# A gated two-branch spectral filter on one core: narrow gate spectra, swaps on the load queue, an inverse in four buffers

## Chip, core and metric

One core of one Trainium2 chip. The metric is device time in microseconds of one launch. A run of the profiler gives the trace that is read here; the times come from runs without it and from that run.

## The reference

`x` is 2048 x 1024 in bf16; `A_w`, `B_w` are complex weights of 2048 x 513; `gate_w` has 1024 elements.

```python
g = sigmoid((x * gate_w).sum(-1, keepdims=True))
a = irfft2(rfft2(x) * (A_w_r + 1j * A_w_i))
b = irfft2(rfft2(x) * (B_w_r + 1j * B_w_i))
return g * a + (1 - g) * b
```

Both branches share the input and its spectrum.

## The kernel before

The transforms are matrix products in seven stages, in one hand-written order. `P.add` records an instruction for one engine with the keys that it reads and writes; each engine's instructions run in the order in which they were recorded, and every DMA has a semaphore of its own. SP issues the loads, ACT issues two small ones. RP is one large buffer of four slots (A0, A1, S0, S1), XF holds spectra.

- Stage 1 (`c` = 0 to 7, two halves `j` each): x in eight pieces of two DMAs, times the constant M, into XF by evictions on ACT or DVE (EV1). x lies in slot A0, M in slot S1.
- The gate needs the sum of x times `gate_w` over a row. It is taken from stage 1's output: `zspec` multiplies XF by the small vectors GS (made from `gate_w`), a DVE product (L411) multiplies the result by the constant E, and `zsum` (L417) adds it up into ZS. `gates` then spreads ZS by matmuls and `sigmoids` (L607) evicts them into FZ. E and the product's result TE also lie in slot S1.
- Stages 2 and 4, for eight row groups `i` (four rows of tiles each): stage 2 is 16 matmuls of 256 columns into PSUM banks 0 to 3, evicted to CG; stage 4 is 8 of 512 columns into banks 4 to 7, evicted to X(i) in XF. The order is 2(0), 2(1), 4(0), 2(2), 4(1) and so on to 2(7), 4(6), 4(7). ACT evicts, with DVE taking half where EVC and EVX name the group.
- The products: `prods(i0, i1, c0, c1)` multiplies, on DVE, spectrum by weights for row groups i0 to i1 and columns c0 to c1. It needs X, and X with even and odd partitions exchanged (a "swap", two DMAs within SBUF into slot S1). For the groups in NSW no swap of X is made; the weights are there in both forms instead.
- Weights: `load_w` lists the loads, `issue_w` issues them on SP. W0 is how many are issued at once; `issue_late` issues those whose place is still in use by x, M or E.
- Stage 5, the inverse over k: 16 units of two column groups `g`, each group 16 matmuls; a unit fills four banks, which ACT evicts in one piece (the call at L648); the last unit is split between ACT and DVE (EV5). Products of later columns are put on DVE between the units (PRODS5), `column0` in front of unit 6 (NCOL0), the unit with groups 0 and 1 at place G0, and `gated` and `rbgen`, which put the gate on the constant U5, near the end.
- Stages 6 and 7, for `r` = 0 to 15: 16 matmuls and an eviction, then the inverse over columns, either whole (8 matmuls of 512 columns, two DVE sums) or, for `r` in FOUR, in quarters (8 of 256 columns, three sums on DVE and one on POOL), and the output DMA.

Before, the swaps of X are issued by POOL (XSQ), and each waits for the sum of the gate:

```python
if i not in NSW:
    for pa in range(2):
        dma(XSQ, sl(RP, S_S1 + 4 * i * RW, [(1, 4 * RW)], p0=pa, np_=64, step=2),
            sl(XF, 4 * i * RW, [(1, 4 * RW)], p0=1 - pa, np_=64, step=2), r=[("X", i), "pad"],
            w=[] if pa else [("XS", i)], a=[("XS", i)] if pa else [], after=[s1, zs[1]] + P.rd["E"])
```

L300 is the line of every matmul, L304 and L305 those of the evictions on ACT and on DVE, L308 that of the products, L291 that of every DMA, L540 that of `rbgen`, L675 that of the sums in stage 7.

Of the kernel before, what the change touches and what calls it, by code (L numbers as in the profile page):

```python
# [4 lines left out]
dt = mybir.dt  # L5
# [23 lines left out]
def make_consts():  # L29
# [23 lines left out]
    E = np.zeros((4, 32, 4, 16, 2, 2, 8))  # L53
    for q in range(4):
        for b in range(2):
            for r in range(8):
                n2 = 32 * b + 8 * q + r
                for t in range(16):
                    if t == 0:
                        re, im = np.ones(32), (-1.0) ** n1  # L60
                    else:
                        ph = pi2 * t * (64 * n1 + n2) / 2048
                        re, im = 2 * np.cos(ph), -2 * np.sin(ph)
                    E[n2 // 16, :, q, t, 0, b, r], E[n2 // 16, :, q, t, 1, b, r] = re / 32, im / 32
    C["E"] = E.reshape(128, 2048)

# [156 lines left out]
def bass_gated_mix__spectral_gfnet__spectral_gfnet__prompt_kernel(nc, A_x, A_w_r, A_w_i, B_x, B_w_r, B_w_i, gate_w, out):  # L223
# [32 lines left out]
    W0 = 36  # L256
    XSQ = "pool"
    NSW = (6, 7)
    ZAT = {5: (0,), 7: (1, 2)}
    ZAT2 = {0: (3,)}  # L260
    ZBANK = (6, 7, 6, 7)
    PRODS = [[], [], [(0, 2, 0, 64)], [(0, 2, 64, 128)], [(2, 4, 0, 64)], [(2, 4, 64, 128)], [(4, 5, 0, 64), (5, 6, 0, 64)], [(6, 7, 0, 64), (7, 8, 16, 32), (7, 8, 32, 64), (7, 8, 0, 16)]]
    PRODS5 = {0: [(4, 8, 64, 128)], 1: [(0, 8, 128, 160)], 2: [(0, 8, 160, 208)], 3: [(0, 8, 208, 248)], 4: [(0, 8, 248, 256)]}
# [12 lines left out]
    POOL7 = range(16)  # L276
    EV5 = (15,)
# [15 lines left out]
    def bank(b):  # L293
        return ("ps", b)
# [18 lines left out]
    MO, MN, EO, TEO = 16, 4112, 8224, 10272  # L313
# [16 lines left out]
    P.add("pool", lambda e: e.memset(sl(XF, 512, [(RW, 32), (1, 16)]), 0.0), w=["pad"])  # L330
    P.add("act", lambda e: e.activation(XST[:, 0:1], sl(XF, 512, [(1, 1)]), ACT.Sigmoid), r=["pad"], w=["XST0"])
# [8 lines left out]
    dma("sp", sl(RP, S_S1 + EO, [(1, 2048)]).bitcast(u16), cst["E"].ap(), w=["E"])  # L340
# [14 lines left out]
    wlist, wlate = [], []  # L355

    def issue_w(n):
        for _ in range(min(n, len(wlist))):
            dst, src, key = wlist.pop(0)
            dma("sp", dst, src, w=[key])  # L360

    def issue_late():
        for dst, src, key in wlate:
            dma("sp", dst, src, w=[key], after=[s1] if key[1] == S_A0 else zs)

    def load_w(t0, n, groups, swapped):

        todo = []
        for f in range(2):
            for ri in range(2):  # L370
                todo.append((f, ri, S_S0 if f == 0 and not swapped else S_A1 if f else S_A0, ri))
                if swapped:
                    todo.append((f, ri, S_S1 if f else S_S0, 1 - ri))
        todo.sort(key=lambda x: x[2] == S_A0)
        for f, ri, base, pa in todo:
            for pm in range(2):
                w = wsrc[f, ri]
                spans = [(t0, n)] if pm == 0 or t0 else [(0, 1), (1, n - 1)]
                for a, m in spans:
                    k1, st = (a, 513) if pm == 0 else (16, 513) if a == 0 else (32 - a, -513)  # L380
                    dst = sl(RP, base + (2 * a + pm) * RW, [(2 * RW, m), (1, 513)], p0=pa, np_=64, step=2)
                    key = ("W", base, pa, pm, a)
                    late = base == S_A0 or base == S_S1 and a < 14
                    (wlate if late else wlist).append((dst, AP(w.tensor, w.offset + k1 * 513, [[32 * 513, 64], [st, m], [1, 513]]), key))
                    for g in groups:
                        wkeys.setdefault(g, []).append(key)

    lo = min(NSW + (8,))
    for g in range(4):
        i0, i1 = 2 * g, min(2 * g + 2, lo)  # L390
        if i0 < i1:
            load_w(2 * i0, 2 * (i1 - i0), range(i0, i1), False)
        if i1 < 2 * g + 2:
            i1 = max(i1, i0)
            load_w(2 * i1, 2 * (2 * g + 2 - i1), range(i1, 2 * g + 2), True)

    issue_w(W0)
    load_ck(*cks[1])
# [4 lines left out]
    def zspec(q):  # L403

        o = ZBANK[q] * 512
        for j in range(2):
            for f in range(4):
                mm(ps(o, [(1, 512)]), sl(GS, 4 * j + f, [(0, 128)]), sl(XF, j * RW + f * 128 + 8 * q, [(2 * RW, 16), (32, 4), (1, 8)]),
                   j == 0 and f == 0, j == 1 and f == 3, ["GS"] + F1[2 * q:2 * q + 2], [bank(ZBANK[q])])
        te = sl(RP, S_S1 + TEO + ((q % 2) * 1024 + (q // 2) * 512) * 2, [(1, 1024)]).bitcast(dt.float32)  # L410
        return P.add("dve", lambda e: e.tensor_tensor(out=te, in0=ps(o, [(1, 512)]), in1=sl(RP, S_S1 + EO + 512 * q, [(1, 512)]), op=ALU.mult),  # L411
                     r=["E", bank(ZBANK[q])], a=[("TE", q % 2)])

    def zsum(q):
        te = sl(RP, S_S1 + TEO + q * 2048, [(1, 2048)]).bitcast(dt.float32)
        src = AP(te.tensor, te.offset, [list(te.ap[0]), [1, 8], [8, 128]])
        return P.add("dve", lambda e: e.tensor_reduce(ZS[:, 8 * q:8 * q + 8], src, mybir.AxisListType.X, ALU.add),  # L417
                     r=[("TE", q)], a=["z"])
# [8 lines left out]
    for c in range(8):  # L427
        if c < 7:
            reverse(c + 1)
        for j in range(2):  # L430
            k = 2 * c + j
            u = k % 3
            for q in range(4):
                r = 4 * c + q
                o = ps(u * 1024 + q * 256, [(1, 256)])
                mo = S_S1 + MO + r * 128
                mm(o, sl(RP, S_A0 + r * 512 + 128 * j, [(1, 128)]), sl(RP, mo, [(8, 16), (0, 2), (1, 8)]), True, False,
                   [("x", c, 0), ("x", c, 1), ("M", MK[c])], [bank(2 * u + q // 2)])
# [5 lines left out]
        for q in ZAT.get(c, ()):  # L444
            zspec(q)
# [18 lines left out]
    def stage4(i):  # L464
# [52 lines left out]
    for what, i in order:  # L517
        if what == "2":
            stage2(i)
            for q in ZAT2.get(i, ()):  # L520
                zspec(q)
            if i == 0:
                zs += [zsum(0), zsum(1)]
                issue_w(len(wlist))
                issue_late()
            continue
# [89 lines left out]
    units = [[g, g + 1] for g in range(2, 32, 2)]  # L616
    units.insert(G0, [0, 1])
    lowlast = max(n for n, gs in enumerate(units) if gs[0] < 16)
    for n, gs in enumerate(units):
# [6 lines left out]
        u = (n + 1) % 2  # L626
        if n == NCOL0:
            column0(4 * u)
        for g in gs:
            if n == 0 and g == gs[1]:  # L630
                gates(12, 4, 0)
                sigmoids(12, 4, 0)
            for q in range(8):
                l0 = 8 * g + q
                for ab in range(2):
                    deps = [("PS" if ab else "PA", g), "CK2"]
                    if g == 0:
                        deps.append(("col0", ab))
                    if g == 31:
                        deps.append(("c256", ab))  # L640
                    w = l0 - 8 * gs[0]
                    last5 = mm(ps(u * 2048 + w * 128, [(1, 128)]), sl(RP, (S_S0 if ab else S_A0) + l0, [(HW, 128)]),
                               sl(CK, KIBo if ab else KIAo, [(1, 128)]), ab == 0, ab == 1, deps, [bank(4 * u + w // 4)])
        if n == lowlast:
            half5 = last5
        parts = [(0, 16)] if n not in EV5 else [(0, 8), (8, 8)]
        for a, cn in parts:
            move("dve" if a else "act", sl(RP, S_A0 + 8 * gs[0] + a, [(HW, 128), (1, cn)]), ps(u * 2048 + 128 * a, [(1, 128), (128, cn)]),  # L648
                 r=banks(4 * u + a // 4, cn // 4), a=["L4"])
# [134 lines left out]
```

## Time and profile before

| | before |
|---|---|
| median of 3 runs (lowest, highest) | 154.51 us (154.02, 154.75) |
| profiled execution | 154.8 us |
| its span, first to last instruction | 152.6 us |
| mean granted TensorE clock | 0.954 |
| busy: PE, DVE, ACT, POOL | 125.3, 104.2, 94.4, 30.0 us |
| DMA | 28.31 MB, mean 185 GB/s |

A row of the timeline or the chain begins with start and length in microseconds; brackets hold the idle time before it and what ended it. A row of a group ends with busy time, mean ns of one, and the idle time before them with its releasers. `SPq` is SP's DMA queue. A row of windows has, behind the five engines' busy times, the granted clock (1.00 is full), the DMA engines' share and GB/s.

### The profile page before, as it was taken

Reading aid. Unit: us, or ns where it says so; the run is one execution under the profiler, and the core shown is the slowest. Engines: PE = TensorE matmul, PEld = TensorE weight load, DVE = VectorE, ACT = ScalarE, POOL = GpSimd, SP = SyncE. Lnnn points to the kernel's source line nnn. Section 1 sums busy time; section 2 is a strip of 40 time slices with the busy share of each in tenths; the row PEclk is TensorE's granted clock in tenths of the full one; section 3 lists DMA queues with packets and bytes.
Section 4 is the critical chain, followed back from the end, with each engine's and each line's share of the span. In section 5 each row is a group of like instructions: output and inputs, shape, how many; then the busy total and the mean of one; then the engine's idle time right before and its main releaser. Section 6 shows DMA issues by size and latency. Waiting matters only on the chain.

```text
span 152.6 us, 3115 instructions
## 1 busy us (share of the span) xinstructions
PE 125.3 (82%) x1293; PEld 98.9 (65%) x1293; DVE 104.2 (68%) x129; ACT 94.4 (62%) x84; POOL 30.0 (20%) x38
## 2 busy tenths in 40 slices
PE   0589999997999995701999959999969998999980
PEld 0358766654665551401999859999966977879630
DVE  1146656369762939248999999995060699989983
ACT  5068643165439999450288936899848786678640
POOL 1000000000442333000000000520000094585840
PEclk9999999999999999975589986999999999999999
DMA  4899999999999999920000000160000113133335
GB/s 102 247 372 362 360 383 350 349 349 352 348 376 389 376 370 420 412 95 0 0 4 0 0 4 0 26 253 0 4 0 4 69 71 137 73 137 142 137 140 206
DMA packets 20016, 28.31 MB, mean 185 GB/s; under 512 B 1697, under 2 KB 16161, under 8 KB 19746
## 3 DMA queue, kind: packets, MB, share of 16 engines
q1 hardware_dynamic: 18896, 24.87, 47.6%
q0 software_dynamic: 960, 3.24, 5.4%
q8 instruction: 10, 0.16, 0.5%
q14 instruction: 4, 0.03, 0.1%
q10 hardware_dynamic: 146, 0.00, 0.1%
HBM read 20.67 MB, written 4.19 MB: 163 GB/s over the span
## 4 chain that ended last, share of the span: by engine, by line
PE 65%; DMA 11%; DVE 8%; ACT 6%; SPq 5%; issue 2%; DVEq 1%; POOL 0%; ACTq 0%
PE PS L300 65%; DMA RP<-XF 7%; SPq L291 5%; DMA RP<-in_A_x_dram 4%; ACT CG L304 4%; DVE ZS L417 3%; DVE RP L308 2%; ACT RP L304 2%; DVE XF L675 2%; DVE RP L305 1%; DVE CG L305 1%; ACT XF L304 1%; DVE RP L411 0%; DVEq L723 0%; POOL RP L291 0%
## 5 line engine op out<-in xcount | busy, mean ns | idle before, releaser
L304 ACT ACTIVATE XF<-PS 128x1024 bf16<-128x1024 f32 (+2 forms) x50 | 46.8, 970 | 21.9 <-PE PS L300 21.2
L300 PE MATMUL PS<-CK,RP 128*128 128x128 bf16 x512 | 36.7, 239 | 8.4 <-DVE RP L308 6.4
L300 PEld LDWEIGHTS PS<-CK,RP 128*128 128x128 bf16 x512 | 35.6, 149 | 9.3 <-DVE RP L308 6.7
L300 PE MATMUL PS<-RP 128*128 128x128 bf16 (+1 forms) x320 | 32.5, 233 | 4.0 <-DMA RP<-in_A_x_dram 1.7
L304 ACT ACTIVATE RP<-PS 128x2048 bf16<-128x2048 f32 (+2 forms) x18 | 29.7, 1678 | 7.6 <-PE PS L300 7.0
L308 DVE TENSOR_TENSOR RP<-XF,RP 128x1024 bf16<-128x1024 bf16 (+9 forms) x31 | 25.0, 843 | 11.9 <-DMA RP<-XF 11.1
L300 PEld LDWEIGHTS PS<-RP 128*128 128x128 bf16 x320 | 22.0, 99 | 7.0 <-issue 2.0
L675 POOL TENSOR_TENSOR XF<-CG 128x512 bf16<-128x512 f32 x10 | 17.7, 1770 | 30.7 <-issue 21.8
L300 PE MATMUL PS<-XF 128*128 128x256 bf16 (+1 forms) x128 | 21.6, 313 | 1.0 <-DVE XF L675 1.0
L304 ACT ACTIVATE CG<-PS 128x2048 bf16<-128x2048 f32 (+1 forms) x8 | 12.5, 1557 | 10.6 <-PE PS L300 10.0
L300 PE MATMUL PS<-FZ,XF 128*128 128x256 bf16 x128 | 15.5, 273 | 2.2 <-ACT CG L304 1.3
L300 PE MATMUL PS<-CG,CK 128*128 128x512 bf16 x64 | 15.2, 380 | 2.0 <-ACT XF L304 2.0
L300 PEld LDWEIGHTS PS<-FZ,XF 128*128 128x128 bf16 x128 | 12.1, 98 | 6.7 <-ACT CG L304 3.3
L300 PEld LDWEIGHTS PS<-XF 128*128 128x128 bf16 x128 | 11.9, 98 | 6.4 <-DVE XF L675 1.3
L300 PE MATMUL PS<-RP,U 128*128 128x256 bf16 x64 | 15.5, 289 | 0.5 <-DVE U L305 0.4
L308 DVE TENSOR_TENSOR RP<-RP 128x2048 bf16<-128x2048 bf16 (+5 forms) x11 | 14.5, 1322 | 0.4
L675 DVE TENSOR_TENSOR CG<-XF,PS 128x512 f32<-128x512 f32 x20 | 12.8, 680 | 2.8 <-ACT XF L304 1.9
L305 DVE CAST XF<-PS 128x1024 bf16<-128x1024 f32 x9 | 11.0, 1221 | 2.1 <-PE PS L300 2.1
L300 PEld LDWEIGHTS PS<-CG,CK 128*128 128x128 bf16 x64 | 5.9, 98 | 8.7 <-ACT XF L304 2.5
L305 POOL COPY RP<-RP 128x512 bf16<-128x512 bf16 x2 | 3.1, 1572 | 37.3 <-DVE RP L308 37.3
L675 DVE TENSOR_TENSOR XF<-XF,PS 128x512 bf16<-128x512 f32 x12 | 7.6, 679 | 4.0 <-PE PS L300 4.0
L305 POOL COPY STAR<-CG 128x2 bf16<-128x2 bf16 x8 | 1.7, 215 | 40.6 <-ACT CG L304 34.7
(39 smaller groups left out, 74.0 us busy)
## 6 DMA issues: line engine op xcount, KB each, us to landing
RP<-in_A_x_dram SPq DMA_DIRECT2D x16, 256.0 KB, 6.2
out_dram<-XF SPq DMA_DIRECT2D x16, 256.0 KB, 2.0
RP<-XF POOLq DMA_DIRECT2D x12, 264.0 KB, 6.0
RP<-in_A_w_r_dram SPq DMA_DIRECT2D x9, 256.5 KB, 7.0
RP<-in_A_w_i_dram SPq DMA_DIRECT2D x9, 256.5 KB, 7.1
RP<-in_B_w_r_dram SPq DMA_DIRECT2D x9, 256.5 KB, 8.1
RP<-in_B_w_i_dram SPq DMA_DIRECT2D x9, 256.5 KB, 7.5
U<-c_U SPq DMA_DIRECT2D x1, 2048.0 KB, 14.9
```

The source lines that it names most:

```text
L291: return P.add(eng, lambda e: e.dma_start(dst, src), dma=True, **kw)
L300: return P.add("pe", lambda e: e.matmul(o, lh, rh, start=start, stop=stop), r=r, w=w)
L304: return P.add("act", lambda e: e.activation(d, s, ACT.Copy), **kw)
L305: return P.add(eng, lambda e: e.tensor_copy(d, s), **kw)
L308: return P.add("dve", lambda e: e.tensor_tensor(out=d, in0=i0, in1=i1, op=ALU.mult), **kw)
L417: return P.add("dve", lambda e: e.tensor_reduce(ZS[:, 8 * q:8 * q + 8], src, mybir.AxisListType.X, ALU.add), r=[("TE", q)], a=["z"])
L675: return P.add(eng, lambda e: e.tensor_tensor(out=od, in0=i0, in1=i1, op=ALU.subtract if h else ALU.add), **kw)
```

## The change

- Gate spectra: each `zspec(h)` runs 16 matmuls with 32 output rows each, for two of four groups of 16 columns, into 32-row quarters of one bank. Two calls (after stage 1, after the first stage 2) take the place of four. E shrinks from 128 x 2048 to 128 x 512, and one product and one reduction over 512 elements take the place of four products and two reductions over 1024.
- Swaps of X for groups 0 to 6 (NSW is now group 7 alone), issued by SP behind the DMAs already issued. Swaps 0 to 5 wait for stage 1, swap 6 for the gate's sum too. 26 portions of weights are issued up front, and then, behind the swap of each group, 4, 4, 4, 4 and 2 more (W1); the rest of the constant CK behind group 3. Group 7's weights are read once and swapped within SBUF (`swap_w`, four DMAs, counted among the portions). U5 is issued behind all of them.
- The first eviction of stage 2 is shared with DVE (EVC).
- Inverse: one column group at a time in four buffers of two banks, evicted in pieces of 8 columns by ACT alone; column 0 is worked out ahead of one more group. Counts of units (NCOL0, NCOPY, G0, NGATE, NRB, PRODS5) are doubled to match.
- r = 0 joins FOUR in stage 7.

The core of the diff:

```diff
-    W0 = 36
-    XSQ = "pool"
-    NSW = (6, 7)
-    ZAT = {5: (0,), 7: (1, 2)}
-    ZAT2 = {0: (3,)}
+    W0 = 26
+    W1 = (4, 4, 4, 4, 2, 0, 0, 0)
+    WCK = 3
+    XSQ = "sp"
+    NSW = (7,)
+    ZAT = 7
...
-    NSTAR3 = 2
-    NCOL0 = 6
-    NCOPY = 8
-    G0 = 7
-    NGATE = {10: 0, 12: 1, 13: 2, 14: 3}
-    NRB = {12: 0, 14: 1}
+    NSTAR3 = 1
+    NCOL0 = 11
+    NCOPY = 14
+    G0 = 14
+    NGATE = {20: 0, 24: 1, 26: 2, 28: 3}
+    NRB = {24: 0, 28: 1}
...
-    EVC = (1, 2, 3)
+    EVC = (0, 1, 2, 3)
-    FOUR = (1, 2, 3, 5, 6, 7, 9, 10, 11, 13)
+    FOUR = (0, 1, 2, 3, 5, 6, 7, 9, 10, 11, 13)
-    EV5 = (15,)
+    EV5 = ()
...
+    def swap_w(src, dst, i):
+        for pa in range(2):
+            o = 4 * i * RW
+            key = ("WS", dst, pa)
+            reads = [k for k in wkeys[i] if k[0] == "W" and k[1] == (src == S_A1)]
+            wlist.append((sl(RP, dst + o, [(1, 4 * RW - 15)], p0=pa, np_=64, step=2),
+                          sl(RP, src + o, [(1, 4 * RW - 15)], p0=1 - pa, np_=64, step=2), key, lambda: dict(r=reads, after=[s1])))
+            wkeys[i].append(key)
...
+    def zspec(h):
         for j in range(2):
             for f in range(4):
+                for g in (h, 2 + h):
+                    mm(ps(3072, [(1, 512)], p0=32 * g, np_=32), sl(GS, 4 * j + f, [(0, 32)]),
+                       sl(XF, j * RW + f * 128 + 16 * g, [(2 * RW, 16), (64, 2), (1, 16)]),
+                       j == 0 and f == 0, j == 1 and f == 3, ["GS"] + F1[4 * h:4 * h + 4], [bank(6)])
...
-                    w=[] if pa else [("XS", i)], a=[("XS", i)] if pa else [], after=[s1, zs[1]] + P.rd["E"])
+                    w=[] if pa else [("XS", i)], a=[("XS", i)] if pa else [], after=[s1] + (zs if i == 6 else []))
+        issue_w(W1[i])
+        if i == WCK:
+            load_ck(*cks[1])
...
-    units = [[g, g + 1] for g in range(2, 32, 2)]
-    units.insert(G0, [0, 1])
+    gorder = list(range(2, G0)) + [0, 1] + list(range(G0, 32))
+    buf = 2
+    for n, g in enumerate(gorder):
...
+        if n == NCOL0:
+            column0(2 * buf)
+            buf = (buf + 1) % 4
...
+        move("dve" if n in EV5 else "act", sl(RP, S_A0 + 8 * g, [(HW, 128), (1, 8)]), ps(buf * 1024, [(1, 128), (128, 8)]),
+             r=banks(2 * buf, 2), a=["L4"])
+        buf = (buf + 1) % 4
```

More of the change, by code (lines that the diff above doesn't have):

```diff
@@ L51, in make_consts @@
     C["M"] = np.concatenate([np.tile(sg.reshape(1, 16) / 4.0, (128, 1)), M.reshape(128, 32 * 128)], axis=1)
[L53 to L65, printed above, removed]
+    E = np.zeros((4, 32, 16, 2, 16))
+    for g in range(4):
+        for r in range(16):
+            for t in range(16):
+                if t == 0:
+                    re, im = np.ones(32), (-1.0) ** n1
+                else:
+                    ph = pi2 * t * (64 * n1 + 16 * g + r) / 2048
+                    re, im = 2 * np.cos(ph), -2 * np.sin(ph)
+                E[g, :, t, 0, r], E[g, :, t, 1, r] = re / 32, im / 32
+    C["E"] = E.reshape(128, 512)
     dd = np.arange(256)[:, None]
@@ L354, in bass_gated_mix__spectral_gfnet__spectral_gfnet__prompt_kernel, with load_w @@
     wkeys = {}
-    wlist, wlate = [], []
+    wlist = []
     def issue_w(n):
         for _ in range(min(n, len(wlist))):
[L359 to L375, printed above, removed]
+            dst, src, key, after = wlist.pop(0)
+            dma("sp", dst, src, w=[key], **after())
+    def load_w(t0, n, f, groups, swapped=False):
+        for ri in range(2):
             for pm in range(2):
@@ L380, in load_w @@
                     k1, st = (a, 513) if pm == 0 else (16, 513) if a == 0 else (32 - a, -513)
[L381 to L384, printed above, removed]
+                    dst = sl(RP, (S_A1 if f else S_S0) + (2 * a + pm) * RW, [(2 * RW, m), (1, 513)],
+                             p0=1 - ri if swapped else ri, np_=64, step=2)
@@ L397, in bass_gated_mix__spectral_gfnet__spectral_gfnet__prompt_kernel @@
+    for g in range(3):
+        for f in range(2):
+            load_w(4 * g, 4, f, (2 * g, 2 * g + 1))
+    load_w(12, 4, 1, (6, 7))
+    load_w(12, 2, 0, (6,))
+    load_w(14, 2, 0, (7,), True)
+    swap_w(S_A1, S_S1, 7)
+    swap_w(S_S0, S_A0, 7)
     issue_w(W0)
-    load_ck(*cks[1])
     F1 = [("F1", c) for c in range(8)]
-    def zspec(q):
-        o = ZBANK[q] * 512
+    def zspec(h):
         for j in range(2):
             for f in range(4):
[L408 to L412, printed above, removed]
@@ L420, in reverse, with zsum @@
+    def zsum():
+        te = sl(RP, S_S1 + TEO, [(1, 1024)]).bitcast(dt.float32)
+        P.add("dve", lambda e: e.tensor_tensor(out=te, in0=ps(3072, [(1, 512)]), in1=sl(RP, S_S1 + EO, [(1, 512)]), op=ALU.mult),
+              r=["E", bank(6)], w=["TE"])
+        src = AP(te.tensor, te.offset, [list(te.ap[0]), [1, 16], [16, 32]])
+        return P.add("dve", lambda e: e.tensor_reduce(ZS[:], src, mybir.AxisListType.X, ALU.add), r=["TE"], w=["z"])
     def reverse(c):
@@ L443, in bass_gated_mix__spectral_gfnet__spectral_gfnet__prompt_kernel @@
             move("dve" if k in EV1 else "act", dst, src, r=banks(2 * u, 2), a=[F1[c]])
[L444 to L445 removed]
+        if c == ZAT:
+            zspec(0)
     def stage2(i):
@@ L625, in bass_gated_mix__spectral_gfnet__spectral_gfnet__prompt_kernel @@
             copies()
-        u = (n + 1) % 2
         if n == NCOL0:
[L628 to L643, printed above, removed]
+            column0(2 * buf)
+            buf = (buf + 1) % 4
+        for q in range(8):
+            l0 = 8 * g + q
+            for ab in range(2):
+                deps = [("PS" if ab else "PA", g), "CK2"]
+                if g == 0:
+                    deps.append(("col0", ab))
+                if g == 31:
+                    deps.append(("c256", ab))
+                last5 = mm(ps(buf * 1024 + q * 128, [(1, 128)]), sl(RP, (S_S0 if ab else S_A0) + l0, [(HW, 128)]),
+                           sl(CK, KIBo if ab else KIAo, [(1, 128)]), ab == 0, ab == 1, deps, [bank(2 * buf + q // 4)])
         if n == lowlast:
             half5 = last5
[L646 to L649, printed above, removed]
+        move("dve" if n in EV5 else "act", sl(RP, S_A0 + 8 * g, [(HW, 128), (1, 8)]), ps(buf * 1024, [(1, 128), (128, 8)]),
+             r=banks(2 * buf, 2), a=["L4"])
+        buf = (buf + 1) % 4
+        if n == 0:
+            gates(12, 4, 0)
+            sigmoids(12, 4, 0)
         if n in NGATE:
```

35 lines of the change are left out of this document (10 added, 25 removed).

## The prediction

> **What bounds the kernel now.** I read the page first, then the chain that ended last in order of time, then the timeline wherever that chain changes engine.
>
> ```profile
> span 152.6 us, 3115 instructions
> ...
> PEclk9999999999999999975589986999999999999999
> ...
> GB/s 102 247 372 362 360 383 350 349 349 352 348 376 389 376 370 420 412 95 0 0 4 0 0 4 0 26 253 0 4 0 4 69 71 137 73 137 142 137 140 206
> ```
>
> A slice is 152.6/40 = 3.8 us. The DMA engines carry 350 to 420 GB/s without a break up to slice 16, which ends at 65 us, and then almost nothing: loads and swaps bound the first 65 us. The TensorE clock falls in two places, around 70 us and around 92 us.
>
> ```profile
> 32.42 3.83 DVE ZS L417 x2
> ...
> 37.45 8.03 PE PS L300 x56
> ...
> 58.07 10.04 DMA RP<-XF
> ...
> 71.83 8.53 PE PS L300 x100
> ...
> 80.46 4.10 PE PS L300 x64
> ...
> 89.30 7.54 PE PS L300 x96
> ...
> 112.94 1.07 PE PS L300 x16
> ```
>
> Start, length, what. Four stretches can be told apart: up to 37.45 (stage 1 and the gate spectra); to 71.83 (stages 2 and 4, closed by a swap of 10 us); to 112.94 (the inverse, stage 5); and the rest (stages 6 and 7). The timeline shows what each hand-over waits for:
>
> ```profile
> 59.31 1.87 ACT L304 ACTIVATE XF<-PS 128x2048 bf16<-128x2048 f32 x1
> ...
> 63.09 0.83 PE L300 MATMUL PS<-CK,ZB 128*128 128x128 bf16 x12
> 63.19 1.88 ACT L304 ACTIVATE XF<-PS 128x2048 bf16<-128x2048 f32 x1 [2.00 <-PE PS L300]
> ...
> 68.24 0.43 DVE L308 TENSOR_TENSOR RP<-XF,RP 128x512 bf16<-128x512 bf16 x1 [2.17 <-DMA RP<-XF]
> ...
> 71.83 1.93 PE L300 MATMUL PS<-CK,RP 128*128 128x128 bf16 x16 [6.44 <-DVE RP L308]
> ...
> 87.39 0.17 PE L300 MATMUL PS<-PST,CK 128*128 128x2 bf16 x1
> ...
> 89.30 22.24 PE L300 MATMUL PS<-CK,RP 128*128 128x128 bf16 x320 [1.75 <-ACT RP L304]
> ```
>
> The last spectrum, X7, is in SBUF at 65.07. The inverse starts 6.8 us later, because the products of row group 5 wait for swap 5 until 68.24.
>
> **The front: gate spectra and their sum.**
>
> ```profile
> 19.39 1.89 PE L300 MATMUL PS<-XF,GS 128*128 128x512 bf16 x8
> 21.11 0.27 PE L300 MATMUL PS<-RP 128*128 128x256 bf16 x1
> ...
> 28.06 1.91 PE L300 MATMUL PS<-FZ,XF 128*128 128x256 bf16 x16
> ...
> 31.73 0.69 DVE L411 TENSOR_TENSOR RP<-PS,RP 128x512 f32<-128x512 f32 x1 [2.78 <-PE PS L300]
> ```
>
> Eight matmuls of a gate spectrum take 21.11 - 19.39 = 1.72 us, 0.215 each (the row's 1.89 holds the end of the last, 0.17, beside which the next ones already run). Before, 32 of them stood on PE in four places. After, there are again 32, each with 512 moving columns but only 32 output rows, 16 after stage 1 and 16 behind the first stage 2. No row shows a 32-row one. Nearest is the 128-row one with the same stream, 0.215, if the two of a pair follow each other; if a pair ran side by side it would be half. I take 0.215.
> Stage 1 no longer stops at 19.39 and ends 1.72 sooner, at 22.9; 16 x 0.215 = 3.44 brings the first stage 2 to 26.3; with its 16 matmuls (1.91 - 0.17 = 1.74) it ends at 28.1, the second gate spectrum at 31.5, the second stage 2 at 33.2, the first stage 4 (8 x 0.215) at 35.0. The next stage 2 began at 37.45 because DVE had 3.83 us of reductions (the chain's first row) in front of its share of an eviction. Now DVE has one product (0.69) and one reduction over half the elements (estimate 1.0, half of one of the two) and is done at 33.2, before that eviction is due. So stage 2 goes on at 35.0: 2.5 us earlier, and X7 is there at 62.6. With pairs side by side it would be 59.2.
> The Trainium skill, TensorEngine Tiling (Array Packing), section Tiling Modes, says that tiles of different output columns work in parallel; by it the gate spectra cost 1.72 us a call and X7 comes at 59.2. No row here shows it, and the next part makes it worth at most 1.5 us.
>
> **The middle: loads and swaps on one queue.**
>
> ```profile
> out_dram<-XF SPq DMA_DIRECT2D x16, 256.0 KB, 2.0
> RP<-XF POOLq DMA_DIRECT2D x12, 264.0 KB, 6.0
> RP<-in_A_w_r_dram SPq DMA_DIRECT2D x9, 256.5 KB, 7.0
> ...
> U<-c_U SPq DMA_DIRECT2D x1, 2048.0 KB, 14.9
> ```
>
> ```profile
> L291 SPq DMA_DIRECT2D RP<-in_A_w_r_dram x11: 607/625/2322, 15.3 to 48.9; - x11
> ```
>
> ```profile
> 52.88 0.69 SPq L291 DMA_DIRECT2D U<-c_U  x1
> ```
>
> The first rows give count, KB and median us from issue to landing; the second fence the time of one issue (least, median, most) and the first and last start. Bytes ahead of the inverse: E falls from 512 to 128 KB, 8 weight transfers of 256 KB go (groups 6 and 7 are no longer read twice), swap 6 and two swaps of weights come (6 x 264 KB): 0.4 + 2.1 - 1.6 = 0.9 MB less. More important is the order: U5 (2 MB) was issued at 52.9 and ran beside swaps 4 and 5; now it stands on SP behind swap 6.
> All that the inverse needs is 4.2 MB of x, 2.4 of constants, 8.4 of weights and 18 swaps of 0.27, 4.9: 19.9 MB. The GB/s row sums to 18.0 MB by 53 us, 19.4 by 57 and 21.0 by 61; at that rate 19.9 MB are there by 58.5 if the queue never runs dry. It is fed as follows. The 26 portions up front, from 15.3 on at 0.62 us or a little over, are issued by about 33. Then each swap waits on SP for its X, and behind that wait are queued four, four, four and two portions, the constants and U5, for which only DVE's products, the star sums and stage 6 wait, later. X0 comes at about 36 (an eviction behind 35.0), with some 0.8 MB still under way, so the waits leave few holes. Swap 6 is issued when X6 is there, at 61.18 - 2.5 = 58.7, in two issues of about 0.6; with 2.0 us to land, as the output's 256 KB, it is there at 61.3, and nothing of U5 is ahead of it.
> DVE then has for row group 6:
>
> ```profile
> L308 DVE TENSOR_TENSOR RP<-XF,RP 128x512 bf16<-128x512 bf16 x7 | 3.0, 422 | 5.0 <-DMA RP<-XF 4.9
> ...
> L308 DVE TENSOR_TENSOR RP<-RP 128x1024 bf16<-128x1024 bf16 x2 | 1.4, 692 | 0.1
> ```
>
> 0.42 + 0.69 + 0.42 and gaps = 1.6, done at 63.1; X7 is there at 62.6, and a first piece of 256 elements (0.3, between the small rows) opens the inverse at **63.5**, against 71.83: 8.3 us earlier, the 2.5 of the front within it. With X7 at 59.2 the loads bind instead, and it starts at about 62. Bounds: 61.5, and 67 if each swap takes the 6 us of its old row.
> POOL's 12 issues and the wait of swaps 0 to 5 for the gate sums go at no price: the path met POOL only through the swaps.
>
> **The inverse.** It took 112.94 - 71.83 = 41.1 us.
>
> ```profile
> 72.00:74.00 2.00, 2.00 (x21) 2.00 (x21) 1.97 (x4) 0.00 (x0) 0.00 (x0) 0.50 0.00 0
> ...
> 78.00:80.00 2.00, 2.00 (x36) 2.00 (x35) 1.97 (x2) 1.56 (x1) 0.00 (x0) 1.00 0.04 8
> ...
> 92.00:94.00 2.00, 2.00 (x22) 2.00 (x21) 1.97 (x2) 1.86 (x1) 0.00 (x0) 0.50 0.00 0
> ```
>
> Behind the eight engine numbers stands the granted clock: 0.50 after each of the two waits of PE. At full clock 64 matmuls take 4.10, 0.064 each. The first 100 took 8.53 instead of 6.4: 2.1 lost. The 96 from 89.30 took 7.54 instead of 6.15: 1.4 lost. The wait between, 87.56 to 89.30, is 1.75.
> That wait goes: column 0 is now worked out one group of eight ahead of its user's two groups, and 1.0 us of matmuls covers most of two copies on ACT; 0.4 stays, and I expect no slow clock behind it (-1.75 + 0.4 - 1.4). At the start PE stands only from about 61.5 to 63.5; a wait of 1.75 was enough for a fall at 89.30, the one before 71.83 was far longer, so I take half of 2.1 as lost, bounds 0 and 2.1 (-1.05). New is that the inverse now starts so close to X7 that the four matmuls which spread the last of the gate (`gates(12, 4, 0)`, behind the first group) wait for the long sigmoid, which reads the same bank until 2.3 us after X7:
>
> ```profile
> L607 ACT ACTIVATE FZ<-PS,SM 128x1536 bf16<-128x1536 f32 x1 | 1.5, 1534 | 0.0
> ...
> L304 ACT ACTIVATE RP<-PS 128x2048 bf16<-128x2048 f32 x15 | 28.2, 1877 | 7.6 <-PE PS L300 7.0
> L304 ACT ACTIVATE RP<-PS 128x1024 bf16<-128x1024 f32 x1 | 1.0, 1018 | 0.0
> ```
>
> That is +1.0 (62.6 + 2.3 against 63.5 + 1.03, and four matmuls). The evictions: 15 of 1.88 and a split one become 32 of 1.02, 32.6 us against 29.2, beside 33 us of matmuls. A group takes PE 16 x 0.064 = 1.03, so ACT just keeps up, and four buffers let it lag three groups. I cost this at nothing; without that slack it is 32 x 0.1 = 3 us. DVE's products, without a break before, go on in the same order with the same number of elements:
>
> ```profile
> 70.22 3.10 DVE L308 TENSOR_TENSOR RP<-XF,RP 128x2048 bf16<-128x2048 bf16 x5 [0.37 <-issue]
> ...
> 96.43 0.70 DVE L308 TENSOR_TENSOR RP<-XF,RP 128x384 bf16<-128x384 bf16 x2
> ```
>
> 26.9 us of DVE stand beside 33 of PE; by their blocks they stay 1 to 3 us ahead of the groups that use them. Sum: 41.1 - 1.75 + 0.4 - 1.4 - 1.05 + 1.0 - 0.2 (the last eviction is shorter) = 38.1, 3.0 less.
>
> **The tail.** r = 0 goes over to the four-quarter form:
>
> ```profile
> 116.10 1.89 PE L300 MATMUL PS<-XF 128*128 128x512 bf16 x8
> ...
> 118.72 1.04 PE L300 MATMUL PS<-XF 128*128 128x256 bf16 x8
> ...
> L675 DVE TENSOR_TENSOR XF<-CG 128x512 bf16<-128x512 f32 x10 | 6.9, 692 | 0.3
> ```
>
> PE saves 0.85, but DVE has 0.69 more to do for r = 0 before r = 1; as r = 0 reaches it earlier too, r = 1 starts about 0.65 sooner, and the rest follows it (bounds 0 and 0.85). POOL's extra product lies beside them.
>
> **The sum.** -8.3 - 3.0 - 0.65 = -12.0 on the profiled execution of 154.8 (span 152.6 and 2.2 around it); that execution is 0.3 above the median, so I take 154.5 - 12.0 = **142.5**.
>
> **The rivals.**
> *The swaps queue up behind weights.* On POOL's queue a swap took 6.0 us with weights under way; on SP's it stands behind every portion issued before it. The Trainium skill, DMA: Bandwidth & Descriptors, section on queues, rings and completion order, says that each engine serves its queues in turn by packets, so the move gives up a turn of its own. The weights' row says 7.0 us to landing. If each swap lands 8 us after its X (7.0 and an issue), swap 6 is there at 66.7, the inverse starts at about 68.6, PE has stood for 7 us and loses the whole 2.1, while the wait at the sigmoid is gone: 3.2 + (3.0 - 1.05 + 1.0) + 0.65 = 6.8 gained, 147.7. For it: the queue is full to 50 us. Against it: less is queued behind X3 than before. 0.12.
> *Slower: SP's order starves the inverse.* The place is SP, held by X4 and by the weights that the two last swaps read; the queue runs dry and swap 6, U5 and the late portions follow one by one. It decides once the inverse starts after 71.83 + 2.95 + 0.65 = 75.4, that is, once swap 6 lands after 73.5 (1.9 of products behind it), 14.8 us after X6. Only U5's 2 MB took as long (14.9). At 18 us the time would be 157.7. 0.04.
> *No change*: the earlier start is lost to ACT at 32 evictions (with 0.3 us between them, 32 x 1.32 = 42 instead of 33) and to the slow clock (2.45): 12.0 - 9.2 - 2.45 = 0.35 gained, 154.2. Of the 7.6 us that ACT sat idle before the 15 long evictions, 7.0 were for PE: 0.04 each is left for anything else. 0.02.
>
> **The numbers.** Forecast, an inverse from 61.5 to 67: 0.82. A measurement of this kernel can tell about 0.5%. The low end takes 61.5, no slow clock, no wait at the sigmoid: 154.5 - 10.3 - 5.1 - 0.85 = 138. The high end reaches through the first rival, with the 0.3 by which the profiled run lies above the median: 148. Faster 0.94, same 0.02, slower 0.04.
>
> **What would show it.** Right: the first stage 2 near 26, the second at 31.5; swap 6 landing before 62; the inverse at 62 to 65 with clock 1.00 throughout or 0.50 once; no wait before column 0's users; stage 6 at about 101.6. Wrong: DVE still waiting for RP<-XF above 66 us, PE waiting for ACT in every group of the inverse, or SP idle on a weight while the DMA row shows a hole before 58 us.

## The result, and the profile after

The changed kernel takes 141.01 us in the median of four runs (139.37 to 141.89), the kernel before 154.26 (153.22 to 154.75): ratio 0.911, 95% interval 0.901 to 0.922. Ratios and intervals here are over the fast runs alone, those within 1.5% of the fastest, while medians and ranges are over all. The profiled execution has a span of 139.7 us. The forecast was 142.5 us (138 to 148).

From the page after, the rows that answer to those of before:

```profile
span 139.7 us, 3146 instructions
...
PEclk9999999999999999995599999999999999999997
...
GB/s 75 258 300 370 349 372 357 350 349 350 363 364 379 363 339 314 412 376 275 5 5 0 0 5 0 5 275 31 0 0 5 81 144 155 75 174 104 113 141 225
```

A slice is now 3.5 us. The DMA engines are full up to slice 17 and part of slice 18, which ends at 66 us, as before, with a dip to 339 and 314 at 49 to 56 us. The end of that stretch is now U5. The clock falls once instead of twice. The chain that ended last, in order of time (start, length, what):

```profile
53.35 1.89 ACT CG L302
...
55.90 5.29 DMA RP<-XF
...
64.93 16.11 PE PS L298 x228
81.04 0.02 issue
81.06 19.54 ACT RP L302 x20
...
100.65 1.08 PE PS L298 x16
```

It still comes through a swap, 5.29 us of it here against 10.04, and then DVE's products. The inverse starts at 64.93 (before: 71.83) and stage 6 at 100.65 (before: 112.94); the tail behind that is 39.0 us (before: 39.7; the page gives spans to 0.1 us). So 6.9 us came ahead of the inverse, 5.4 within it (35.7 against 41.1) and 0.7 behind. The timeline after, at the same places as before:

```profile
23.38 1.90 PE L298 MATMUL PS<-XF,GS 128*32 128x512 bf16 x16
25.22 1.92 PE L298 MATMUL PS<-FZ,XF 128*128 128x256 bf16 x16
...
29.11 0.69 DVE L410 TENSOR_TENSOR RP<-PS,RP 128x512 f32<-128x512 f32 x1 [0.64 <-PE PS L298]
29.84 1.02 DVE L413 TENSOR_REDUCE ZS<-RP 128x16 f32<-128x512 f32 x1
...
58.73 0.42 DVE L306 TENSOR_TENSOR RP<-XF,RP 128x512 bf16<-128x512 bf16 x1 [1.89 <-DMA RP<-XF]
...
58.99 1.88 ACT L302 ACTIVATE XF<-PS 128x2048 bf16<-128x2048 f32 x1 [2.00 <-PE PS L298]
...
61.31 0.42 DVE L306 TENSOR_TENSOR RP<-XF,RP 128x512 bf16<-128x512 bf16 x1 [0.97 <-DMA RP<-XF]
...
64.93 1.93 PE L298 MATMUL PS<-CK,RP 128*128 128x128 bf16 x16 [3.73 <-DVE RP L306]
...
78.69 0.17 PE L298 MATMUL PS<-PST,CK 128*128 128x2 bf16 x1
...
78.71 20.82 PE L298 MATMUL PS<-CK,RP 128*128 128x128 bf16 x336
```

Sixteen narrow gate matmuls take 25.22 - 23.38 = 1.84 us, little more than eight wide ones (1.72). The trace has the start of each: they come in pairs, the two of a pair 3 to 4 ns apart and the next pair 0.216 us later. X7 is in SBUF at 60.87, 4.2 us earlier; the products of row group 5 wait for swap 5 until 61.31 and those of group 6 follow. At column 0 (78.69) PE doesn't wait at all.

SP's queue shows why swap 5 is late although X5 is there at 53.1:

```profile
51.54 1.12 SPq L289 DMA_DIRECT2D RP<-XF  x2
52.83 1.56 SPq L289 DMA_DIRECT2D RP<-RP  x2
54.44 3.69 SPq L289 DMA_DIRECT2D RP<-XF  x4
58.17 0.58 SPq L289 DMA_DIRECT2D U<-c_U  x1
```

Swap 4, two swaps of weights, swaps 5 and 6, U5. Swap 5 landed at 61.19 and swap 6 at 62.47. The median landing times, with U5 behind everything:

```profile
RP<-XF SPq DMA_DIRECT2D x14, 264.0 KB, 5.5
U<-c_U SPq DMA_DIRECT2D x1, 2048.0 KB, 9.5
```

### The profile page after: what moved, and what is told of

It reads as the page before. It is cut to its first block, busy times and chain, and to the rows that moved or that the text cites. A ratio compares the mean times of both kernels' runs of the same rounds, so it can differ in the third digit from the quotient of the medians.

```text
span 139.7 us, 3146 instructions
## 1 busy us (share of the span) xinstructions
PE 118.5 (85%) x1293; PEld 95.0 (68%) x1293; DVE 100.8 (72%) x128; ACT 95.7 (69%) x100; POOL 26.3 (19%) x28
## 4 chain that ended last, share of the span: by engine, by line
PE 60%; ACT 20%; DMA 8%; DVE 4%; SPq 3%; issue 2%; DVEq 1%; ACTq 0%
PE PS L298 60%; ACT RP L302 14%; ACT CG L302 5%; DMA RP<-in_A_x_dram 4%; DMA RP<-XF 4%; SPq L289 3%; DVE RP L306 2%; DVE XF L667 2%; ACT XF L302 1%; DVEq L715 0%; DVE U L303 0%; DVEq L212 0%; ACTq L212 0%
## 5 line engine op out<-in xcount | busy, mean ns | idle before, releaser
L298 PE MATMUL PS<-CK,RP 128*128 128x128 bf16 x512 | 33.8, 231 | 3.7 <-DVE RP L306 3.7
L298 PEld LDWEIGHTS PS<-CK,RP 128*128 128x128 bf16 x512 | 33.3, 147 | 3.9 <-DVE RP L306 3.8
L302 ACT ACTIVATE RP<-PS 128x1024 bf16<-128x1024 f32 (+1 forms) x34 | 32.1, 998 | 5.0 <-PE PS L298 4.8
L306 DVE TENSOR_TENSOR RP<-XF,RP 128x1024 bf16<-128x1024 bf16 (+9 forms) x32 | 23.1, 756 | 8.9 <-DMA RP<-XF 8.4
L667 POOL TENSOR_TENSOR XF<-CG 128x512 bf16<-128x512 f32 x11 | 19.5, 1771 | 22.8 <-issue 13.7
L667 DVE TENSOR_TENSOR CG<-XF,PS 128x512 f32<-128x512 f32 x22 | 14.1, 680 | 7.6 <-ACT XF L302 6.8
L302 ACT ACTIVATE CG<-PS 128x1024 bf16<-128x1024 f32 (+1 forms) x8 | 11.6, 1451 | 9.7 <-PE PS L298 9.1
L306 DVE TENSOR_TENSOR RP<-RP 128x2048 bf16<-128x2048 bf16 (+6 forms) x12 | 16.8, 1402 | 0.4
L303 POOL COPY STAR<-CG 128x2 bf16<-128x2 bf16 x8 | 2.7, 334 | 52.1 <-DVE CG L303 37.3
L303 DVE COPY U<-RP 128x1024 bf16<-128x1024 bf16 x8 | 3.4, 426 | 8.3 <-DMA RP<-in_A_x_dram 8.3
```

Of the source, the lines that this page charges most:

```text
L298: return P.add("pe", lambda e: e.matmul(o, lh, rh, start=start, stop=stop), r=r, w=w)
L302: return P.add("act", lambda e: e.activation(d, s, ACT.Copy), **kw)
L303: return P.add(eng, lambda e: e.tensor_copy(d, s), **kw)
L306: return P.add("dve", lambda e: e.tensor_tensor(out=d, in0=i0, in1=i1, op=ALU.mult), **kw)
L667: return P.add(eng, lambda e: e.tensor_tensor(out=od, in0=i0, in1=i1, op=ALU.subtract if h else ALU.add), **kw)
```

## The experiments

My theory after the result: the bytes ahead of the swaps on the queue hold the start of the inverse, the narrow gate spectra count only as far as they let swaps leave earlier, and the four buffers account for most of what the inverse gained. The rivals: the swaps' new queue brings the gain; DVE or the spectra hold the start; the inverse only profits from a better clock. All times below are medians; spans and places are from the profiled execution of each.

**Pairs of narrow matmuls one behind the other.**

```diff
-        for j in range(2):
-            for f in range(4):
-                for g in (h, 2 + h):
+        for g in (h, 2 + h):
+            for j in range(2):
+                for f in range(4):
```

> The changed kernel, with the 16 gate matmuls of each call in another order: all eight of one 32-row quarter, then all eight of the other, so that neighbours no longer lie in different quarters. In the changed kernel 16 take 1.84 us (23.38 to 25.22 in its trace), half of what I had counted. If the pairs ran side by side because they alternate, each call now takes about 3.44 us, the last spectrum X7 comes 3.2 us later (60.87 to about 64) and the inverse, which swaps 5 and 6 hold back to 64.93, starts about 1.5 us later (66.4): about 142.5 us. Rival: narrow matmuls cost half whatever their order; then the call still takes 1.84 us and the time stays at 141.

142.93 us (142.68 to 143.70), ratio 0.929 [0.924, 0.934], against 0.911 [0.901, 0.922] for the changed kernel.

The timeline of PE:

```profile
22.67 2.78 PE L298 MATMUL PS<-XF,GS 128*32 128x512 bf16 x16
25.39 1.92 PE L298 MATMUL PS<-FZ,XF 128*128 128x256 bf16 x16
```

From start to the next start it is 25.39 - 22.67 = 2.72 us a call, against 1.84. So the order matters, but neither theory's number is met: eight of one quarter and then eight of the other are dearer by half, not by double. The starts in the trace show why: four pairs still start 5 to 17 ns apart and eight matmuls start alone, twelve steps of 0.216 us, 2.6 in all. That the four pairs are the end of the first quarter beside the beginning of the second is my reading; the trace doesn't name the quarters. The start of the inverse moved to 65.86, by 0.9. X7 came at 63.57, 2.7 later; two calls explain 2 x 0.88 = 1.8 of that, and the last stage 4 took 3.57 us there instead of 1.91, at a low clock.

**Swaps on POOL's queue, U5 behind swap 6.**

```diff
-    XSQ = "sp"
+    XSQ = "pool"
-    ... cst["U5"].ap(), w=["U5"], after=[s1])
+    ... cst["U5"].ap(), w=["U5"], after=[s1] + P.wr[("XS", 6)])
```

> The changed kernel with the swaps of X issued by POOL again; U5 waits until swap 6 has landed, so that only the queue of the swaps differs. If it was the order (U5 last) that brought the gain and the queue matters little, the inverse starts within 1.5 us of 64.93, earlier rather than later, since in the changed kernel SP is so busy issuing that swaps 3 to 5 leave 1.4 to 2.4 us after their spectrum is there: 139.5 to 141.5 us. Rival: the place between the portions of weights is what brings the swaps in; then they land later on POOL's queue, the inverse starts at 67 or later, and the time is 143 us or more.

138.35 us (138.12 to 139.43), ratio 0.900 [0.894, 0.906]. The inverse started at 64.17, but X7 had come late there (63.28), and DVE no longer waited for a swap after 54 us:

```profile
53.85 0.69 DVE L306 TENSOR_TENSOR RP<-XF,RP 128x1024 bf16<-128x1024 bf16 x1 [2.85 <-DMA RP<-XF]
...
64.17 1.18 PE L298 MATMUL PS<-CK,RP 128*128 128x128 bf16 x16 [0.56 <-DVE RP L306]
```

The rival falls: with U5 last, the swaps' place on the load queue is no part of the gain. Whether it costs something was left to a comparison on one chip, below.

**U5 ahead of swaps 4 to 6.**

```diff
         if i == WCK:
             load_ck(*cks[1])
+            dma("sp", U5[:].bitcast(u16), cst["U5"].ap(), w=["U5"], after=[s1])
...
-    dma("sp", U5[:].bitcast(u16), cst["U5"].ap(), w=["U5"], after=[s1])
```

> The changed kernel with the 2 MB load of U5 moved ahead, behind the rest of the constant CK in group 3, so that swaps 4 to 6 stand behind it on the queue. If the queue's bytes hold the start of the inverse, it comes 2.1 MB at 0.37 MB per us = 5.6 us later, less what the queue stood part empty (about 1 us): 69.5, and the time is 145.5 us. Rival: the queue has room, and the spectra or DVE's products hold the start; then it moves by less than 2 us, 141 to 143 us.

146.33 us (146.13 to 147.14), ratio 0.951 [0.946, 0.957]: 5.3 us above the changed kernel's median, near the 4.5 that the bytes gave.

```profile
63.90 0.42 DVE L306 TENSOR_TENSOR RP<-XF,RP 128x512 bf16<-128x512 bf16 x1 [7.59 <-DMA RP<-XF]
66.50 0.43 DVE L306 TENSOR_TENSOR RP<-XF,RP 128x512 bf16<-128x512 bf16 x1 [0.99 <-DMA RP<-XF]
...
70.13 1.93 PE L298 MATMUL PS<-CK,RP 128*128 128x128 bf16 x16 [8.94 <-DVE RP L306]
```

DVE waits 7.59 us for swap 4, where it waited 1.89, and PE starts at 70.13, 5.2 later. X7 was there at 60.85: the spectra don't hold it.

**The old inverse in the changed kernel.**

```diff
-    for n, g in enumerate(gorder):
...
-            column0(2 * buf)
-            buf = (buf + 1) % 4
...
+    for n, gs in enumerate(units):
...
+        u = (n + 1) % 2
...
+            column0(4 * u)
...
+        parts = [(0, 16)] if n not in EV5 else [(0, 8), (8, 8)]
+        for a, cn in parts:
```

(with it, the counts of units and the pieces of the products go back)

> The changed kernel with the inverse of the kernel before: units of two column groups in two buffers of four banks, column 0 directly ahead of the unit before its user, the last eviction split. All else stays. The inverse took 41.1 us before and 35.7 after (64.93 to 100.65). If the four buffers bring it, it goes back to about 39.5 (1.75 waiting at column 0, 1.4 of slow clock behind that, about 1 of small waits), and the time is 145 us. Rival: most of the 5.4 us came from the earlier start and the better clock in front; then the inverse stays under 37 us, and the time is 141 to 142.

145.03 us (143.16 to 146.24), ratio 0.945 [0.938, 0.951]. The inverse runs from 63.11 to 102.01, 38.9 us against 35.7 (34.5 to 36.2 in the other nine profiles with four buffers):

```profile
63.11 1.18 PE L298 MATMUL PS<-CK,RP 128*128 128x128 bf16 x16 [1.57 <-DVE RP L306]
...
79.79 20.81 PE L298 MATMUL PS<-CK,RP 128*128 128x128 bf16 x320 [1.74 <-ACT RP L302]
...
102.01 1.95 PE L298 MATMUL PS<-RP 128*128 128x128 bf16 x32 [1.41 <-DVE RP L303]
```

The wait at column 0 is back with 1.74 us. The slow clock that followed it before is not: its window reads

```profile
80.00:82.00 2.00, 2.00 (x36) 2.00 (x35) 2.00 (x3) 0.00 (x1) 0.00 (x0) 1.00 0.04 8
```

So some 3.2 us of the 5.4 belong to the buffers and column 0's place. Of the other 2.2, the second slow clock was 1.4, and its fall isn't a consequence of that wait alone.

**Only U5 last, in the kernel before.**

```diff
-    dma("sp", U5[:].bitcast(u16), cst["U5"].ap(), w=["U5"], after=[s1])
+    dma("sp", U5[:].bitcast(u16), cst["U5"].ap(), w=["U5"], after=[s1] + P.wr[("XS", 5)])
```

> The kernel before, with one dependency more: the load of U5 waits until swap 5 has landed. Nothing else of the change. If U5's 2 MB beside swaps 4 and 5 held the start of the inverse (their last landed at 68.1, about 9.5 us after issue), swap 5 now lands near 64 and the inverse starts at 67.5 to 68.5 instead of 71.83, set by X7 (65.07) and DVE's products behind it: about 150.5 us, 4 less than before. Rival: the weights that are read twice and the swaps themselves fill the queue to there; then the start moves by less than 1.5 us, 153 us or more.

148.67 us (147.82 to 150.65), ratio 0.965 [0.959, 0.971]. Expected was 150.5. One dependency gives about two fifths of the whole gain (3.5 of 8.9 per cent).

```profile
62.78 0.33 SPq L291 DMA_DIRECT2D U<-c_U  x1
...
63.31 1.88 ACT L304 ACTIVATE XF<-PS 128x2048 bf16<-128x2048 f32 x1 [2.00 <-PE PS L300]
...
66.91 1.39 PE L300 MATMUL PS<-CK,RP 128*128 128x128 bf16 x16 [1.39 <-DVE RP L308]
```

U5 is issued at 62.78, when swap 5 has landed: 5.0 us after its issue (57.67) instead of 10.6. The inverse starts at 66.91, 1.7 us behind X7.

**Only the narrow gate, in the kernel before.**

```diff
-        for q in ZAT.get(c, ()):
-            zspec(q)
+        if c == 7:
+            zspec(0)
...
-                zs += [zsum(0), zsum(1)]
+                zspec(1)
+                zs.append(zsum())
```

> The kernel before, with the narrow gate spectra, the small E and the single product and reduction alone. X7 then comes 3 to 4 us earlier (65.07 to about 61.5). If the queue holds the inverse, as I think, its start follows only by the 0.39 MB of E (1 us) and by what the earlier spectra let swaps 4 and 5 start sooner (up to 3.5 us): it starts at 68.5 to 70.5, and the time is 151 to 153 us. Rival: the start follows the spectra in full (67.6); then about 150 us.

146.15 us (145.70 to 146.63), ratio 0.953 [0.948, 0.957]; expected were 151 to 153, and even the rival's 150 was too much. The inverse starts at 64.00, 7.8 us earlier, more than X7's 3.9. The queues show how:

```profile
49.33 1.07 POOL L289 DMA_DIRECT2D RP<-XF  x2 [0.81 <-ACT XF L302]
...
53.26 1.07 POOL L289 DMA_DIRECT2D RP<-XF  x2 [1.81 <-ACT XF L302]
53.35 0.72 SPq L289 DMA_DIRECT2D U<-c_U  x1
...
64.00 1.93 PE L298 MATMUL PS<-CK,RP 128*128 128x128 bf16 x16 [2.46 <-DVE RP L306]
```

Swap 4 leaves 4 us ahead of U5 and swap 5 beside it; in the kernel before both left after U5's 52.88, at 53.60 and 57.54. Swap 5 landed at 60.25 instead of 68.12: four microseconds of spectra bought eight of landing. U5 beside it on the other queue cost swap 5 little (6.1 and 6.5 us to land for its two DMAs); U5 ahead of it had cost more (8.7 and 10.0).

This run also bounds the rest of the front. With the narrow gate alone the inverse starts at 64.00, as early as with the whole change (63.1 to 64.9 in four profiles). No run here shows that U5's place, the swaps' queue or the fewer loads of weights bring the start further forward once the gate is narrow; the run with U5 ahead shows that, on SP's queue, U5 must not stand before the swaps.

**Six of SP's DMAs on POOL.**

```diff
-            dma("sp", dst, src, w=[key], **after())
+            dma("pool" if key[0] == "WS" else "sp", dst, src, w=[key], **after())
-    load_ck = lambda o, n, k: dma("sp", ...
+    load_ck = lambda o, n, k: dma("pool" if o else "sp", ...
```

> The changed kernel with six of SP's DMAs issued by POOL instead: the four swaps of group 7's weights and the rest of the constant CK. In the changed kernel SP issues swaps 3, 4 and 5 only 1.7, 2.4 and 1.4 us after their spectrum, and the GB/s row dips to 339 and 314 at 49 to 56 us. If SP's row of waits and issues costs this, swap 5 leaves at 53.1 instead of 54.4, the dip goes, the inverse starts 1 to 2.5 us earlier (62.5 to 64), and the time is 138.5 to 140 us. Rival: the bytes hold it, whoever issues them, or POOL's issues come later; then the start stays within 0.7 us of 64.93 and the time within 0.7 of 141.

140.22 us (138.66 to 140.98), ratio 0.911 [0.904, 0.918], that of the changed kernel. In the profile, which is of the fastest of the four runs, swap 5 left at 53.17, as forecast, and landed at 58.29 instead of 61.19; DVE waited for no swap after 53 us. But X7 only came at 62.49, and the inverse started at 62.99:

```profile
62.99 1.21 PE L298 MATMUL PS<-CK,RP 128*128 128x128 bf16 x16 [0.17 <-DVE RP L306]
```

So with SP's row of issues gone, it is X7 and the clock in the last stage 4 that hold the start. 62.99 lies hardly under the 63.1 to 64.9 of the four profiles with SP's issues, and over the runs nothing is gained that can be told.

**r = 0 whole.**

```diff
-    FOUR = (0, 1, 2, 3, 5, 6, 7, 9, 10, 11, 13)
+    FOUR = (1, 2, 3, 5, 6, 7, 9, 10, 11, 13)
```

> The changed kernel with r = 0 of stage 7 in its old whole form. The stretch from the start of stage 6 to the end of the span was 39.66 us before and 39.05 after. If the 0.6 between them comes from r = 0, it goes back to 39.6 to 39.7 and the time rises by 0.6, to about 141.6. Rival: it comes from the clock or from the second set of products in place of the split eviction; then the stretch stays at 39.0 to 39.2.

```profile
99.73 1.96 PE L298 MATMUL PS<-RP 128*128 128x128 bf16 x32 [1.12 <-ACT RP L302]
```

Stage 6 starts at 99.73 and the span ends at 139.4: 39.7 us, as long as before, against 39.0. So from the changed kernel's side the tail's 0.7 is r = 0. It is worth that only beside the unsplit last eviction: the run with the old inverse, which has r = 0 in quarters and the split eviction, has a tail of 141.4 - 102.01 = 39.4. There DVE waits 1.24 us for PE at the last row, where it waits 0.87 in the changed kernel; why, the trace doesn't say. The median of 141.76 (140.99 to 143.17) has too wide a spread to add to that.

**The changed kernel and three versions on one chip.**

> The changed kernel once more, for a comparison on one chip with the three that follow: 141 us, spread by 1 to 2 us with the time at which the clock falls.

> Swaps by POOL and U5 behind swap 6, again, on the same chip as the changed kernel. If the queue of the swaps costs the change 2 to 3 us, as the first run of it suggests, this is at 138 to 139 us and at least 1.5 us under the changed kernel beside it. Rival: the difference was between chips and the place of the slow clock; then the two are within 1 us.

> Swaps by POOL and U5 behind swap 6, and the last eviction of the inverse split again, four columns on ACT and four on DVE. The wait of stage 6 for it was 1.12 us; half the elements take 0.6, so it falls to about 0.7, and the time is 0.4 under the kernel without the split. Rival: DVE comes late from the gate's products; then nothing is gained.

> As the last, and the four matmuls that spread the last of the gate go into another bank ahead of the inverse, with their sigmoid. In the run with swaps by POOL, the inverse started 0.9 us behind X7 and then waited 0.35 us for the sigmoid, and these matmuls took 0.25. If both lie on the path there, it gains 0.5 us more, about 137.5 us. Rival: two sigmoids ahead of the first eviction hold ACT back by 0.7 us, the four buffers take that up, and the gain is under 0.3.

```diff
+        for a, cn in ([(0, 8)] if n < 31 else [(0, 4), (4, 4)]):
+            move("dve" if a else "act", ... 8 * g + a ..., ps(buf * 1024 + 128 * a, [(1, 128), (128, cn)]), ...)
...
     star2()
+    gates(12, 4, 1536)
     sigmoids(0, 12, 0)
+    sigmoids(12, 4, 1536)
...
-        if n == 0:
-            gates(12, 4, 0)
-            sigmoids(12, 4, 0)
```

(the first two lines in both of the last kernels, the rest in the last)

| | median, range us | ratio to before, interval | inverse starts | stage 6 starts |
|---|---|---|---|---|
| changed, again | 140.01 (139.19 to 141.35) | 0.910 [0.906, 0.915] | 64.90 | 100.13 |
| swaps by POOL, U5 last | 139.40 (138.05 to 140.53) | 0.904 [0.899, 0.909] | 63.95 | 98.50 |
| and last eviction split | 138.93 (137.95 to 139.60) | 0.904 [0.900, 0.907] | 62.53 | 98.02 |
| and gate spread early | 139.30 (138.01 to 139.77) | 0.905 [0.901, 0.910] | 63.90 | 98.60 |

On one chip the swaps' queue, with U5 behind swap 6, is worth 0.6 us in the medians, which the intervals don't separate: the rival's case. The first run's 2.7 us, a difference between two sets of runs, didn't repeat. POOL's queue was the lower one both times, so a small gain isn't excluded. The split eviction shortens stage 6's wait from 1.12 to 0.88 us, little more than half of what was expected, because DVE's half ends last; and its tail is again 39.4 us instead of 39.0, which takes the gain back. The early gate gains nothing. The split version has the lowest median, 1.1 us under the changed kernel beside it, with intervals that overlap, and its profile doesn't show the split to be the reason.

## Why the prediction was right, point by point

**The start of the inverse: 63.5 forecast, 64.93 measured** (63.1, 63.7 and 64.9 in three more profiles with the same front). The mechanism held: the swaps end ahead of the inverse, and the earlier spectra and U5's place bring them in. Two sizes were wrong and met in the middle, which is luck. The narrow matmuls were counted at 0.215 and take 0.115, since the two of a pair run side by side: the first stage 2 came at 25.2 instead of 26.3, the second at 28.9 instead of 31.5 and X7 at 60.9 instead of 62.6. The Trainium skill, TensorEngine Tiling (Array Packing), section Tiling Modes, has it that such tiles work in parallel; the trace agrees, with 1.84 us for 16 where the prediction worked out 1.72 by that page, and 2.72 when they were put one behind the other. Against that, the 2.0 us to land, taken from the output rows, was 5.5 for a swap: the DMA engines were full, and the 6 us of the swaps' old row, which I had kept for the bound, was the nearer value. The chain goes through swap 5, which SP reached 1.4 us after X5. Swap 6, on which the forecast hung, was hardly earlier: issued at 57.02 instead of 58.7, it landed at 62.47 instead of 61.3, while DVE was busy with row group 5 until 62.56. That is past the 62 given as a sign of being right.

By the working of the prediction, matmuls side by side should have brought X7 at 59.2. Half of the missing 1.7 us is a misread row of the kernel before:

```profile
35.50 1.04 PE L300 MATMUL PS<-FZ,XF 128*128 128x256 bf16 x8
37.45 1.05 PE L300 MATMUL PS<-FZ,XF 128*128 128x256 bf16 x8 [0.92 <-DVE CG L305]
```

The row at 37.45 is the second half of that stage 2. The forecast 35.0 was for the start of the first half, and its eight matmuls, 0.9 us, lie between: the front's gain was counted 0.9 us too high. The other 0.8 is there by the time this stage 2 starts, at 32.40: stage 1 ended 0.5 later than forecast, and the two calls took 0.12 more each.

I was also wrong to treat the front as hidden behind the loads, worth at most another 1.5 us. Alone, in the kernel before, it moved the start by 7.8 us, and U5's order alone by 4.9; together with the swaps on SP they give 6.9. They remove the same hold, the late landing of swaps 4 and 5, so their gains don't add.

**The inverse: 38.1 forecast, 35.7 measured.** Of the terms: the wait at column 0 went entirely (0.4 had been left); the second slow clock went (the run with the old inverse shows that it can stay away with the wait still there); the last eviction is shorter. The wait at the sigmoid (+1.0) didn't occur, as the inverse started 4 us behind X7, not 1. The first slow clock, of which I had kept half, is all there: 20 matmuls take 2.15 us from 64.93 to 67.08 and the next 160 11.00, where 0.062 each would make 1.24 and 9.9, so 2.0 is lost. And a term was missing: matmuls at full clock take 20.82/336 = 0.062 instead of 0.064, because PE no longer waits a little for its buffer, 1.1 us over 512. In the kernel before, neighbouring matmuls start 0.06 us apart, but 0.2 to 0.3 at every second unit. ACT keeps up, as forecast:

```profile
70.28 30.31 ACT L302 ACTIVATE RP<-PS 128x1024 bf16<-128x1024 f32 x32 [0.23 <-PE PS L298]
```

32 evictions in a row, 0.95 each, two of them column 0's. The chain names ACT for its last 19.5 us, but PE ends its last group only one eviction ahead of stage 6; neither waits for the other for long. The rest of the difference, under 1 us, I can't place.

**The tail: -0.65 forecast, -0.7 measured**, and shown to be r = 0, beside an unsplit last eviction.

The total is nearer than its parts: 8.3, 3.0 and 0.65 were forecast, 6.9, 5.4 and 0.7 came.

**The rivals.** The swaps did queue behind weights. The 8 us of the first rival, counted from X, is about what swaps 0 to 5 took (6.4 to 9.5 us; swap 5 took 8.1). It failed at the one that it was put on: swap 6 landed 5.5 us after X6, with only swap 5 issued just before it. The swaps on POOL's queue again were worth 0.6 us, which the intervals don't separate. What the Trainium skill, DMA: Bandwidth & Descriptors, section Queues, rings and completion order, says of queues served in turn would have made the move to SP's queue lose a turn; the runs show no price beyond these 0.6 us. SP's order starved nothing: at 339 and 314 GB/s beside some 363 the queue lost (24 + 49)/363 x 3.5 = 0.7 us. "No change" was refuted by the inverse, where 32 evictions in a row took ACT 30.31 us, and not 42.

## What to carry to other kernels

When a chain ends in a transfer, look at which larger transfer left just before it that nobody needs yet: in the kernel before, making 2 MB wait for a 264 KB swap brought the inverse 4.9 us forward with one dependency. Two changes that remove the same wait don't add, so price each alone against the wait, not against the sum. A finer ring of buffers pays twice, in the waits that it removes and in the small ones of every turn that no row of the chain shows.

## What the runs showed of the hardware

Where the clock falls is a matter of the run, not only of the kernel. Every profile has PE waiting 2.03 us ahead of the last stage 4. In the changed kernel's first profile the clock stayed at 1.00 behind it and fell to 0.50 in the later wait for the swaps (3.73 us). In its second profile it fell at once; the window and the timeline of PE there:

```profile
58.00:60.00 2.00, 2.00 (x6) 0.74 (x7) 1.23 (x3) 0.00 (x0) 0.00 (x0) 0.56 0.87 350
```

```profile
57.93 3.32 PE L298 MATMUL PS<-CG,CK 128*128 128x512 bf16 x8 [2.03 <-ACT XF L302]
```

The granted clock (third from the right) is 0.56, and the last stage 4 takes 3.32 us instead of 1.91. Shifts like this one are part of the spread of about 2 us between runs of one kernel. At column 0 it is the same: behind a wait of about 1.75 us the clock fell in the kernel before and in both versions of it with one part of the change, and stayed at 1.00 when the same inverse stood in the changed kernel (the window of 80 to 82 us above).

The traces tell where. In all fourteen, once the clock has first risen, it changes only at whole multiples of 3.41 us from its other changes: it was at 0.50 for 6.83 us from 62.69 in the changed kernel, and for 10.24 us from 66.87 and 3.41 from 90.76 in the kernel before. Every fall ends a step of 3.41 us in which PE was busy at most 0.58 of the time. No step with 0.59 or more was followed by a fall, every step under 0.40 was, and between them both occur. In the second profile the wait ahead of the last stage 4 lies whole in the step from 54.83 to 58.24, where PE was busy for 1.33 us. In the first the steps cut it in two, with 2.57 and 2.22 us busy, and the clock stayed. At column 0 the step had 1.66 us busy in the kernel before, and 1.75 where the old inverse stood in the changed kernel.

The Trainium skill, TensorE: Matmul & The Clock Gate, section Part 1, has a window of about 3.4 us that runs freely, whatever the kernel does, and has the clock fall after an idle window. The traces agree with the first. They differ on the second: steps in which PE was idle for about half of the time were enough here. Where a step begins is given by the run, and no run here could choose it.
